# Gated linear recurrence and gated unit: 1024-token chunks, the gated input on GpSimd, the scan fed from PSUM, quarter-array convolution, 4 KB transfers

## Chip, cores, metric

The kernel runs on one core of a Trainium2 chip. The metric is the device time of one execution in microseconds, as the median of several. The kernel before takes 374.9 us (374.4 to 377.2 in three runs).

Engines are named as in the profile: PE is TensorE (PEld its weight loads), DVE is VectorE, ACT is ScalarE, POOL is GpSimd, SP issues the DMAs.

## The reference, cut to what matters

```python
B, S, D = 4, 6336, 256                      # 25,344 tokens, fp32 in and out
# recurrence, per channel
log_a = 8.0 * sigmoid(r_gate) * log(clip(sigmoid(a_param), 1e-6, 1 - 1e-6))
a     = exp(log_a)
xg    = sqrt(max(1 - a * a, 1e-6)) * sigmoid(i_gate) * x
h[t]  = a[t] * h[t-1] + xg[t]               # restarts at each of the 4 sequences
# gated unit on h
gate  = sigmoid(sum_k conv_w[k] * h[t - 4 + k])   # causal, 5 taps, per channel
out   = (gate * (h @ w_val)) @ w_out
```

Both kernels compute the sigmoids through tanh: sigmoid(z) is 0.5 * (1 + tanh(z / 2)).

## The kernel before: the parts that matter

Tokens go through in windows of 512. Inputs arrive with tokens on the partitions. The recurrence needs channels on the partitions, so TensorE transposes; u and tanh of r are transposed, and everything after that is channel-major. A list scheduler inside the kernel writes the order of the instructions.

```python
# loads: four rows of 1 KB per partition
nc.sync.dma_start(dst, src[t0:t0 + nj * P, :].rearrange("(j p) d -> p j d", p=P))
# tanh of both gates
nc.scalar.activation(out=tri, in_=ri, func=ACT.Tanh, scale=0.5)
# u = (1 + tanh_i) * x: one DVE instruction, both inputs in SBUF
nc.vector.scalar_tensor_tensor(out=uring, in0=tri[:, 1], scalar=1.0, in1=xt, op0=ALU.add, op1=ALU.mult)
# a = exp(k * tanh_r + k), read from the transposed PSUM tile, written densely
nc.scalar.activation(out=aring[.., h, 0:n], in_=srT[:, h, 0:n], func=ACT.Exp, scale=khf, bias=khf)
# a * a on GpSimd, then the square root on ACT
nc.gpsimd.tensor_tensor(out=ering, in0=a, in1=a, op=ALU.mult)
nc.scalar.activation(out=nring, in_=ering, func=ACT.Sqrt, scale=-0.25, bias=b025)
# xg = uT (PSUM) * norm (SBUF); then the scan, both tensor inputs in SBUF
nc.vector.tensor_tensor(out=xg, in0=uT, in1=nh, op=ALU.mult)
nc.vector.tensor_tensor_scan(out=yb, data0=aring, data1=xg, initial=.., op0=ALU.mult, op1=ALU.add)
# convolution: ten matmuls of 128x128 diagonal weights, 512 wide
nc.tensor.matmul(out=gp[:, h, c0:c1], lhsT=diag[:, h, kk, :], rhs=yb[:, h, o:o + c1 - c0], ..)
```

Of the kernel before, what the change touches and what calls it, by code (L numbers as in the profile page):

```python
# [8 lines left out]
P = 128  # L9
WIN = 512  # L10
SUB = WIN // P
CONV_K = 5
C_SCALE = 8.0
NS = 11
NY = 7
NIN = 3
NTRI = 3
NOSB = 3
MIN_UNIT = [1, 2, 3, 4]
COST = dict(load=4.5, tanh=1.9, u2=1.3, srT=0.5, uT=0.5, exp=1.45, e=2.15, xg=0.66, scan=2.7, conv=2.4, tg=0.97,  # L20
            val=0.95, gv=1.16, out=0.47, osbD=0.64, osbA=0.62, sq=0.88, sq0=0.2, table=1.3, store=1.5,
            sem=0.15, dma=2.2)
FP32 = mybir.dt.float32
# [5 lines left out]
def make_plan(frac):  # L29




    nw = len(frac)
    nq = [max(1, round(2 * f)) for f in frac]
    qwin = [(g, i) for g in range(nw) for i in range(nq[g])]
    qlast = [sum(nq[:g + 1]) - 1 for g in range(nw)]
    done, nxt, free = {}, {}, {}
    order, units = [], []
    mode = "E"  # L40

    def at(op):
        return nxt.get(op, 0)

    while True:
        cands = []

        def cand(op, eng, dur, deps, prio, i, n=1):
            t = 0.0
            for d in deps:  # L50
                if d[1] < 0:
                    continue
                if d not in done:
                    return
                t = max(t, done[d] + COST["sem"])
            if eng == "ACT" and op != "osb" and (op == "sq") != (mode == "S"):
                dur = dur + COST["table"]
            cands.append((max(free.get(eng, 0.0), t), prio, op, eng, dur, i, n))

        def per_window(op, eng, prio, deps, limit=nw):  # L60
            g = at(op)
            if g < limit:
                cand(op, eng, COST[op] * frac[g], [(d, g + o) for d, o in deps], prio, g)

        nsq = at("sq")
        per_window("load", "DMA", 0, [("tanh", -NIN), ("u2", -NIN)])
        per_window("tanh", "ACT", 3, [("load", 0), ("srT", -NTRI), ("u2", -NTRI)])
        per_window("u2", "DVE", 0, [("tanh", 0), ("uT", -NS)])
        per_window("srT", "PE", 0, [("tanh", 0), ("exp", -2)])
        per_window("exp", "ACT", 1, [("srT", 0), ("scan", -NS), ("e", -NS)])  # L70
        per_window("e", "POOL", 0, [("exp", 0), ("xg", -NS)])
        per_window("uT", "PE", 1, [("u2", 0), ("xg", -1)], nsq)
        per_window("xg", "DVE", 3, [("uT", 0), ("sq", 0), ("scan", -1)], nsq)
        per_window("scan", "DVE", 2, [("xg", 0), ("val", -NY)], nsq)
        per_window("conv", "PE", 3, [("scan", 0), ("tg", -1)])
        per_window("tg", "ACT", 0, [("conv", 0), ("gv", -2)])
        per_window("val", "PE", 2, [("conv", 0), ("gv", -1)])
        g = at("gv")
        if g < nw:
            cand("gv", "DVE", COST["gv"] * frac[g],  # L80
                 [("tg", g), ("val", g), ("out", qlast[g - 2] if g >= 2 else -1)], 1, g)
        q = at("out")
        if q < len(qwin):
            cand("out", "PE", COST["out"], [("gv", qwin[q][0]), ("osb", q - 1)], 1, q)
        q = at("osb")
        if q < len(qwin):
            for e, eng in (("D", "DVE"), ("A", "ACT")):
                cand("osb", eng, COST["osb" + e], [("out", q), ("store", qwin[q][0] - NOSB)], 0.5, q)
        g = at("store")
        if g < nw:  # L90
            cand("store", "DMA", COST["store"] * frac[g], [("osb", qlast[g])], -1, g)

        n = at("e") - nsq
        if n and mode == "E":
            all_in = at("exp") == nw
            stuck = at("e") == at("exp") and (all_in or ("scan", at("exp") - NS) not in done
                                              and at("exp") >= NS)
            low = (nsq - at("scan")) * (COST["xg"] + COST["scan"]) <= 2 * COST["table"] + COST["sq"] * n
            enough = n >= min(MIN_UNIT[min(len(units), len(MIN_UNIT) - 1)], nw - nsq)
            if stuck or (low and enough):  # L100
                cand("sq", "ACT", COST["sq0"] + COST["sq"] * sum(frac[nsq:nsq + n]),
                     [("e", nsq + n - 1)], -1, nsq, n)
        if not cands:
            break
        t, prio, op, eng, dur, i, n = min(cands)
        free[eng] = t + dur
        order.append((t, op, i, eng, n))
        nxt[op] = i + n
        for k in range(i, i + n):
            done[(op, k)] = t + dur + (COST["dma"] if eng == "DMA" else 0.0)  # L110
        if op == "sq":
            units.append(n)
        if eng == "ACT" and op != "osb":
            mode = "S" if op == "sq" else "E"
    assert at("store") == nw
    order.sort(key=lambda o: o[0])
    return order, qwin
# [3 lines left out]
def kernel(  # L121
# [15 lines left out]
    T = B * S  # L137

# [4 lines left out]

    nwin = (T + WIN - 1) // WIN
    ntok = [min(WIN, T - g * WIN) for g in range(nwin)]

    segs = []
    for g in range(nwin):
        t0, t1 = g * WIN, g * WIN + ntok[g]
        cuts = [t0] + [c for c in range(S, T, S) if t0 < c < t1] + [t1]  # L150
        segs.append([(c0 - t0, c1 - t0, c0 % S == 0) for c0, c1 in zip(cuts[:-1], cuts[1:])])
    YW = WIN + 4 * max(len(s) for s in segs)

    plan, qwin = make_plan([n / WIN for n in ntok])

    const = ctx.enter_context(tc.tile_pool(name="const", bufs=1))
    inp = ctx.enter_context(tc.tile_pool(name="inp", bufs=3))
    live = {}

    def load(g):  # L160
        nj = ntok[g] // P
        t0 = g * WIN
        ri = inp.tile([P, 2, SUB, D], FP32, name="ri", tag="ri", bufs=NIN)
        xt = inp.tile([P, SUB, D], FP32, name="xt", tag="xt", bufs=NIN)
        for dst, src in ((ri[:, 0, 0:nj, :], rf), (ri[:, 1, 0:nj, :], if_), (xt[:, 0:nj, :], xf)):
            nc.sync.dma_start(dst, src[t0:t0 + nj * P, :].rearrange("(j p) d -> p j d", p=P))
        live["ri", g], live["xt", g] = ri, xt

    with tc.manual_schedule():
        ap2 = const.tile([H, P], FP32, name="ap2")  # L170
        nc.sync.dma_start(ap2[:], a_param.rearrange("(h p) -> h p", p=P))
        wrow = const.tile([CONV_K, D], FP32, name="wrow")
        nc.sync.dma_start(wrow[:], moe_conv_w[:, :])
        for g in range(NIN):
            load(g)
# [7 lines left out]
        wv = const.tile([P, H, D], BF16, name="wv")  # L183
        nc.gpsimd.dma_start(wv[:], moe_w_val.rearrange("(hk p) n -> p hk n", p=P))
        wo = const.tile([P, H, D], BF16, name="wo")
        nc.gpsimd.dma_start(wo[:], moe_w_out.rearrange("(hk p) n -> p hk n", p=P))
        khf = const.tile([P, H], FP32, name="khf")
        wcol = const.tile([P, H, CONV_K], FP32, name="wcol")
        with tc.tile_pool(name="ps_setup", bufs=1, space=bass.MemoryType.PSUM) as ps_setup:
            kps = ps_setup.tile([P, H], FP32, name="kps")  # L190
            nc.tensor.transpose(out=kps[:], in_=ap2[0:H, :], identity=ident_f[0:H, 0:H])
            kt = const.tile([P, H], FP32, name="kt")
            nc.scalar.activation(out=kt[:], in_=kps[:], func=ACT.Tanh, scale=0.5)
            ksig = const.tile([P, H], FP32, name="ksig")
            nc.vector.tensor_scalar(out=ksig[:], in0=kt[:], scalar1=0.5, scalar2=0.5,
                                    op0=ALU.mult, op1=ALU.add)
            nc.vector.tensor_scalar(out=ksig[:], in0=ksig[:], scalar1=1e-6, scalar2=1.0 - 1e-6,
                                    op0=ALU.max, op1=ALU.min)
            kln = const.tile([P, H], FP32, name="kln")
            nc.scalar.activation(out=kln[:], in_=ksig[:], func=ACT.Ln)  # L200
            nc.vector.tensor_scalar(out=khf[:], in0=kln[:], scalar1=0.5 * C_SCALE, scalar2=None, op0=ALU.mult)
            wc_ps = ps_setup.tile([P, H, CONV_K], FP32, name="wc_ps")
            for h in range(H):
                nc.tensor.transpose(out=wc_ps[:, h, :], in_=wrow[0:CONV_K, h * P:(h + 1) * P],
                                    identity=ident_f[0:CONV_K, 0:CONV_K])
            nc.vector.tensor_copy(out=wcol[:], in_=wc_ps[:])
# [25 lines left out]
        def op_load(g, eng, n):  # L232
            if g >= NIN:
                load(g)
# [176 lines left out]
```

## Time and profile before

| | before |
|---|---|
| median time | 374.9 us |
| profiled span | 372.5 us |
| DVE busy | 334.6 us |
| ACT busy | 312.4 us |
| PE busy | 272.4 us |
| POOL busy | 138.3 us |
| DMA queue's share of 16 engines | 85.7% |

The busy line of the profile counts, for each engine, the time in which it works on an instruction. A group's line gives the source line, the engine and operation, what it writes and reads, how often, then the total busy time and the mean length of one in ns, then the idle time just before such instructions and who ended it. The lines on which the argument rests are in the prediction below.

These are the groups by shape of the kernel before; the second number behind the bar is the mean in ns.

```profile
L257 ACT ACTIVATE aring<-srT,khf 128x512 f32<-128x512 bf16 x98 | 70.7, 795 | 3.4 <-PE srT L228 2.2 <-issue 1.2
...
L257 ACT ACTIVATE aring<-srT,khf 128x256 f32<-128x256 bf16 x2 | 1.0, 562 | 0.0
```

### The profile page before, as it was taken

The numbers are of one execution on the slowest core, as the hardware profiler recorded it, in microseconds if no ns is written. First come the engines' busy times: TensorE is split into PE (matmuls) and PEld (weight loads), VectorE is DVE, ScalarE is ACT, GpSimd is POOL, SyncE is SP. The second block draws the span as 40 slices with busy tenths as digits, with TensorE's granted clock in tenths as the row PEclk, the third lists the DMA queues.
The fourth block names the chain that finished last, engine by engine and source line by source line (L and its number), as shares of the span: only waits on it lengthen the run. The fifth ranks groups of instructions, "written<-read, shape, count | busy, mean of one in ns | idle before, by whom it ended". The sixth has DMA issues, their size and how long they took to land.

```text
span 372.5 us, 5299 instructions
## 1 busy us (share of the span) xinstructions
PE 272.4 (73%) x1933; PEld 159.9 (43%) x1933; DVE 334.6 (90%) x326; ACT 312.4 (84%) x298; POOL 138.3 (37%) x111
## 2 busy tenths in 40 slices
PE   0362779877686969877677887696976696869994
PEld 0232445444445535434344454363543363435543
DVE  3363999999999979999999999999999999999982
ACT  4898899999998799998967989789997997873342
POOL 2234435634362726434425324451655056300000
PEclk9995699999899899999889989789999899999998
DMA  8999996999999989996889979979999895313333
GB/s 210 355 348 353 356 350 201 298 353 339 345 361 324 330 268 361 352 364 202 280 264 339 351 226 295 356 255 344 301 323 336 278 340 187 127 56 114 113 114 141
DMA packets 105160, 104.42 MB, mean 280 GB/s; under 512 B 3240, under 2 KB 105135, under 8 KB 105135
## 3 DMA queue, kind: packets, MB, share of 16 engines
q1 hardware_dynamic: 104590, 103.83, 85.7%
q0 software_dynamic: 544, 0.26, 0.5%
q8 instruction: 15, 0.25, 0.3%
q14 instruction: 11, 0.08, 0.1%
HBM read 78.39 MB, written 25.95 MB: 280 GB/s over the span
## 4 chain that ended last, share of the span: by engine, by line
DVE 34%; ACT 23%; issue 19%; PE 14%; DMA 5%; POOL 2%; DVEq 0%; ACTq 0%
DVE yring L306 13%; DVE uring L246 8%; DVE gv L344 7%; ACT tri L240 6%; ACT ering L277 5%; PE gp L321 5%; PE ops L356 4%; ACT aring L257 4%; DMA xt<-in_x_dram 3%; DVE xg L290 3%; PE val L338 3%; ACT tg L327 3%; DVE osb L367 2%; ACT L327 2%; ACT L277 2%
## 5 line engine op out<-in xcount | busy, mean ns | idle before, releaser
L262 POOL TENSOR_TENSOR ering<-aring 128x1024 f32<-128x1024 f32 (+1 forms) x50 | 105.7, 2121 | 140.9 <-ACT aring L257 121.8
L321 PE MATMUL gp<-yring,diag 128*128 128x512 bf16 (+4 forms) x530 | 124.5, 384 | 24.7 <-DVE yring L306 14.2
L306 DVE TENSOR_TENSOR_SCAN yring<-aring,yring,xg 128x512 bf16<-128x512 f32 (+4 forms) x98 | 139.5, 1464 | 0.7
L240 ACT ACTIVATE tri<-ri 128x2048 bf16<-128x2048 f32 (+1 forms) x50 | 94.4, 1907 | 0.0
L321 PEld LDWEIGHTS <-diag 128*128 128x128 bf16 x530 | 50.8, 102 | 83.5 <-issue 16.3
L356 PE MATMUL ops<-wo,gv 128*128 128x256 bf16 x396 | 61.8, 280 | 26.2 <-DVE gv L344 12.4
L257 ACT ACTIVATE aring<-srT,khf 128x512 f32<-128x512 bf16 (+1 forms) x100 | 71.8, 791 | 3.4 <-PE srT L228 2.2
L246 DVE SCALAR_TENSOR_TENSOR uring<-tri,xt 128x1024 bf16<-128x1024 bf16 (+1 forms) x50 | 67.4, 1356 | 7.0 <-ACT tri L240 6.9
L327 ACT ACTIVATE tg<-gp 128x1024 bf16<-128x1024 f32 (+1 forms) x50 | 51.1, 1023 | 25.7 <-PE gp L321 21.2
L344 DVE SCALAR_TENSOR_TENSOR gv<-tg,val 128x1024 bf16<-128x1024 bf16 (+1 forms) x50 | 59.7, 1194 | 2.5 <-PE val L338 1.7
L304 POOL COPY yring<-yring 128x8 bf16<-128x8 bf16 x49 | 31.6, 644 | 77.4 <-DVE yring L306 77.4
L356 PEld LDWEIGHTS <-gv 128*128 128x128 bf16 x396 | 36.7, 99 | 50.0 <-DVE gv L344 20.2
L338 PE MATMUL val<-yring,wv 128*128 128x512 bf16 (+4 forms) x212 | 52.1, 371 | 5.3 <-DVE gv L344 5.3
L228 PE MATMUL srT<-ident_b,tri 128*128 128x128 bf16 x396 | 33.4, 232 | 22.2 <-ACT tri L240 22.2
L277 ACT ACTIVATE ering<-ering,b 128x3072 bf16<-128x3072 f32 (+2 forms) x21 | 47.0, 2280 | 0.1
L369 ACT COPY osb<-ops 128x512 f32<-128x512 f32 x46 | 27.2, 592 | 22.2 <-PE ops L356 19.1
L367 DVE COPY osb<-ops 128x512 f32<-128x512 f32 x53 | 36.1, 682 | 9.2 <-PE ops L356 8.0
L228 PE MATMUL uT<-ident_b,uring 128*128 128x128 bf16 x396 | 33.3, 232 | 15.0 <-DVE xg L290 14.7
L228 PEld LDWEIGHTS <-tri 128*128 128x128 bf16 x396 | 27.0, 104 | 33.2 <-ACT tri L240 27.1
L290 DVE TENSOR_TENSOR xg<-uT,ering 128x1024 bf16<-128x1024 bf16 (+1 forms) x50 | 33.7, 675 | 6.2 <-ACT ering L277 6.2
L228 PEld LDWEIGHTS <-uring 128*128 128x128 bf16 x396 | 28.3, 104 | 20.0 <-issue 14.3
L338 PEld LDWEIGHTS <-wv 128*128 128x128 bf16 x212 | 19.9, 99 | 18.9 <-issue 6.6
(31 smaller groups left out, 53.3 us busy)
## 6 DMA issues: line engine op xcount, KB each, us to landing
ri<-in_r_gate_dram SPq DMA_DIRECT2D x49, 512.0 KB, 6.1
ri<-in_i_gate_dram SPq DMA_DIRECT2D x49, 512.0 KB, 7.4
xt<-in_x_dram SPq DMA_DIRECT2D x49, 512.0 KB, 7.3
out_dram<-osb SPq DMA_DIRECT2D x49, 512.0 KB, 4.6
ri<-in_r_gate_dram SPq DMA_DIRECT2D x1, 256.0 KB, 7.0
ri<-in_i_gate_dram SPq DMA_DIRECT2D x1, 256.0 KB, 7.2
xt<-in_x_dram SPq DMA_DIRECT2D x1, 256.0 KB, 6.6
out_dram<-osb SPq DMA_DIRECT2D x1, 256.0 KB
```

The costliest lines, as they stand in the source:

```text
L228: nc.tensor.transpose(out=dst[:, h, j * P:(j + 1) * P], in_=src[:, j, h * P:(h + 1) * P], identity=ident_b[:])
L240: nc.scalar.activation(out=tri[:, :, 0:nj, :], in_=ri[:, :, 0:nj, :], func=ACT.Tanh, scale=0.5)
L246: nc.vector.scalar_tensor_tensor(out=uring[:, g % NS, 0:nj, :], in0=tri[:, 1, 0:nj, :], scalar=1.0, in1=xt[:, 0:nj, :], op0=ALU.add, op1=A ...
L257: nc.scalar.activation(out=aring[:, g % NS, h, 0:ntok[g]], in_=srT[:, h, 0:ntok[g]], func=ACT.Exp, scale=khf[:, h:h + 1], bias=khf[:, h:h ...
L262: nc.gpsimd.tensor_tensor(out=ering[:, g % NS, :, 0:ntok[g]], in0=a, in1=a, op=ALU.mult)
L277: nc.scalar.activation(out=nring[:, sl:sl + k, 0:H * WIN], in_=ering[:, sl:sl + k].rearrange("p s h t -> p s (h t)"), func=ACT.Sqrt, scale ...
L306: nc.vector.tensor_tensor_scan(out=yb[:, h, o:o + c1 - c0], data0=aring[:, g % NS, h, c0:c1], data1=xg[:, h, c0:c1], initial=0.0 if fresh ...
L321: nc.tensor.matmul(out=gp[:, h, c0:c1], lhsT=diag[:, h, kk, :], rhs=yb[:, h, o:o + c1 - c0], start=(kk == 0), stop=(kk == CONV_K - 1))
L327: nc.scalar.activation(out=tg[:, :, 0:ntok[g]], in_=live.pop(("gp", g))[:, :, 0:ntok[g]], func=ACT.Tanh, scale=0.5)
L338: nc.tensor.matmul(out=val[:, m, c0:c1], lhsT=wv[:, hk, m * P:(m + 1) * P], rhs=yb[:, hk, o:o + c1 - c0], start=(hk == 0), stop=(hk == H - 1))
L344: nc.vector.scalar_tensor_tensor(out=gv[:, :, 0:ntok[g]], in0=live.pop(("tg", g))[:, :, 0:ntok[g]], scalar=1.0, in1=live.pop(("val", g))[: ...
L356: nc.tensor.matmul(out=ops[:, e, :], lhsT=gv[:, hk, p0:p0 + P], rhs=wo2[:, hk, :], start=(hk == 0), stop=(hk == H - 1))
```

## The change

The intent is to take work off the DVE, the busiest engine, to free what remains there of waiting for GpSimd, and to make transfers longer:

- u moves to GpSimd (from the fifth chunk on). There, a pass that adds one comes first and a plain product second.
- The product with the norm is formed in token order: the norm is transposed instead of u, the product is transposed by a matmul into fp32 PSUM, and the scan reads it there.
- The convolution uses 64x64 tiles of the array, four at a time.
- Partitions hold four consecutive tokens, so that a transfer's packet is 4 KB. Access patterns with a stride put the tokens in order again: in exp's output, in the norm's transposes, in the transposes ahead of the scan and in the output matmul.
- Chunks of 1024 tokens, a fixed list of instructions in place of the scheduler, PSUM banks assigned by hand.

The diff, cut to its core:

```diff
-            nc.sync.dma_start(dst, src[t0:t0 + nj * P, :].rearrange("(j p) d -> p j d", p=P))
+        return dram[start[c] + o:start[c] + o + n, :].rearrange("(p q) d -> p q d", q=n // P)
 ...
-            nc.vector.scalar_tensor_tensor(out=uring[..], in0=tri[:, 1, ..], scalar=1.0,
-                                           in1=xt[..], op0=ALU.add, op1=ALU.mult)
+        def op_s1(k, bank):
+            t = tri[:, c % NRI, 1, 0:CHUNKS[c] * H]
+            nc.gpsimd.tensor_scalar(out=t, in0=t, scalar1=1.0, scalar2=0.0, op0=ALU.add, op1=ALU.add)
+        def op_u(k, bank):
+            if c in U_DVE:          # chunks 0 to 3
+                nc.vector.scalar_tensor_tensor(out=u, in0=t, scalar=1.0, in1=xt, op0=ALU.add, op1=ALU.mult)
+            else:
+                nc.gpsimd.tensor_tensor(out=u, in0=t, in1=xt, op=ALU.mult)
 ...
+                src = src.rearrange("c (s q p) -> c s q p", p=P, q=q)
+                dst = dst.rearrange("c (s p q) -> c s q p", p=P, q=q)
+            nc.scalar.activation(out=dst, in_=src, func=ACT.Exp, ..)
 ...
+            nc.vector.tensor_tensor(out=v, in0=u, in1=nn, op=ALU.mult)     # v is u; nn: the transposed norm, in PSUM
+                    dst = pp[..].rearrange("c (p q) -> c q p", q=q)
+                        nc.tensor.matmul(out=dst[:, j, :], lhsT=u[..], rhs=ident_b[:], start=True, stop=True)
-                        data0=aring[..], data1=xg[:, h, c0:c1],
+            nc.vector.tensor_tensor_scan(out=yring[..], data0=aring[..], data1=pp[..], initial=prev, ..)
 ...
-                        nc.tensor.matmul(out=gp[:, h, c0:c1], lhsT=diag[:, h, kk, :], ..)
+                    for r, h, col in QUADS:
+                        nc.tensor.matmul(out=pp[col * HP:(col + 1) * HP, ..],
+                                         lhsT=diag[r * HP:(r + 1) * HP, h, kk, :], ..)
 ... (the fixed plan, buffers, setup: left out)
```

## The prediction

> **What bounds the kernel now.** I read the page's busy shares first, then the busy time in stretches of the span, then the groups of instructions by shape inside two of those stretches, then the timeline of two engines side by side. The busy line and the stretches:
>
> ```profile
> PE 272.4 (73%) x1933; PEld 159.9 (43%) x1933; DVE 334.6 (90%) x326; ACT 312.4 (84%) x298; POOL 138.3 (37%) x111
> ...
> q1 hardware_dynamic: 104590, 103.83, 85.7%
> ```
>
> ```profile
> 20.00:40.00 20.00, 9.99 (x68) 6.09 (x67) 11.12 (x11) 18.81 (x16) 7.71 (x5) 0.73 1.10 353
> 40.00:320.00 280.00, 216.94 (x1569) 127.47 (x1568) 272.03 (x249) 255.50 (x243) 123.15 (x86) 0.95 0.95 307
> 320.00:360.00 40.00, 34.42 (x227) 18.82 (x226) 39.10 (x43) 20.02 (x22) 3.25 (x11) 1.00 0.27 93
> ```
>
> The columns of the stretches are PE, weight loads, DVE, ACT and POOL busy, the granted clock, the DMA share and GB/s. From 40 to 360 us the DVE is busy 311.1 of 320 us: it is the bound. The DMA is nearly as full (0.95) until 320 us and then falls to 0.27: loads run up to eleven windows ahead, so the last 40 us are DVE work alone. Why the DVE needs 334.6 us shows in the scan, first between 100 and 280 us, then after 330 us, when GpSimd makes no more squares:
>
> ```profile
> L306 DVE TENSOR_TENSOR_SCAN yring<-aring,yring,xg 128x512 bf16<-128x512 f32 x48 | 74.4, 1590 | 0.4
> L246 DVE SCALAR_TENSOR_TENSOR uring<-tri,xt 128x1024 bf16<-128x1024 bf16 x27 | 37.1, 1380 | 0.4 <-ACT tri L240 0.4
> L344 DVE SCALAR_TENSOR_TENSOR gv<-tg,val 128x1024 bf16<-128x1024 bf16 x26 | 31.3, 1205 | 1.9 <-PE val L338 1.1 <-ACT tg L327 0.8
> ```
>
> ```profile
> L306 DVE TENSOR_TENSOR_SCAN yring<-aring,yring,xg 128x512 bf16<-128x512 f32 x12 | 14.7, 1267 | 0.0
> L344 DVE SCALAR_TENSOR_TENSOR gv<-tg,val 128x1024 bf16<-128x1024 bf16 x8 | 9.6, 1200 | 0.2 <-PE val L338 0.2
> L306 DVE TENSOR_TENSOR_SCAN yring<-aring,yring,xg 128x256 bf16<-128x256 f32 x2 | 1.4, 739 | 0.0
> ```
>
> The same 512-wide scan takes 1267 ns alone and 1590 ns on average beside GpSimd; gv does not change (1200 and 1205). The timelines of DVE and of POOL from 164 us show one case, two scans under two squares, 5.75 us instead of 2.5:
>
> ```profile
> 164.95 5.75 DVE L306 TENSOR_TENSOR_SCAN yring<-aring,yring,xg 128x512 bf16<-128x512 f32 x2
> ```
>
> ```profile
> 164.97 4.66 POOL L262 TENSOR_TENSOR ering<-aring 128x1024 f32<-128x1024 f32 x2 [2.15 <-ACT aring L257]
> ```
>
> **What the Trainium skill says.** (1) "SBUF — State Buffer", section "Who interferes with whom": a DVE instruction with two SBUF inputs contends with a GpSimd instruction that reads SBUF, the loser waits for the whole instruction, and one with at most one SBUF input does not contend. The trace agrees: scan and u (two SBUF inputs each) stretch, gv, xg and the output copy (one input from PSUM) keep 1205, 680 and 682 ns whether GpSimd works or not. (2) "DMA: Bandwidth & Descriptors", section "Why small descriptors are slow": a fixed cost per packet; its ceiling for 16 engines is 435 GB/s ("Where 436 GB/s comes from"). Packets of 1 KB took 46 ns at the median here (356 GB/s over 16 engines), 50 on average, which fits. (3) "TensorEngine Tiling (Array Packing)", section "Key Properties": four 64x64 tiles run in parallel, and changing the mode drains the array. The trace before has no tiles, so nothing here shows it. (4) "SBUF — State Buffer", section "Door 1", on cachelines: a stride beyond 16 bytes in SBUF or beyond 8 in PSUM costs rate. Before, everything is contiguous; no row shows it.
>
> **The change, part by part.** Units are tokens: 25,344 of them, two elements per token and partition.
>
> *DVE.* u leaves for GpSimd in all but the first four chunks: 50 x 1.35 = 67.4 us become about 6.4 (676, 1209, and twice 2276 ns by the same slope). The scan reads the coefficient from SBUF and the input from fp32 PSUM, so its lock is gone, and 1024 tokens go in one instruction: 739 ns at 256 and 1267 at 512 give 2.06 ns per element, so 2.32 us for 1024; 46 x 2.32 + 4 x 1.27 + 6 x 0.74 = 116 us, against 139.5. The product xg still has one SBUF and one PSUM operand in bf16, 48 x 0.68 + 3 x 0.42 = 34. gv is untouched, 60. Output copies: 36 of 1024 elements on the DVE (0.68 at 512, so about 1.22) = 44, against 36. With setup the DVE has 265 us instead of 334.6.
>
> *GpSimd.* Squares alone last 1892 ns for 1024 and 1038 for 512 elements: 1.67 ns per element and 0.18 fixed. 46 x 1.89 + 4 x 1.04 + 6 x 0.61 = 95 us. u at the same two-input rate is 3.60 us per 1024-token chunk, 21 such and three smaller: 80. The added "plus one" pass over the same tiles has one input; between half and the whole of u's rate: 43 to 80. The small copies of four columns (31.6 us, mostly waiting for the lock) go. Sum 218 to 255 us: 58 to 68% of the old span, off the bound.
>
> *ACT.* The same functions in longer instructions: tanh 1060 ns at 1024 and 1925 at 2048 give 3.66 at 4096, so 23 x 3.66 + 2 x 1.93 + 3 x 1.06 = 91 (94.4 before); exp 562 at 256, 795 at 512, so about 1.23 at 1024, 46 x 1.23 + 4 x 0.80 + 6 x 0.56 = 63 (71.8); square roots 16 instructions at 0.84 ns per element plus 0.27 each = 47; tg 51; 12 full output copies of 1.02 and two half ones = 13 (27.2); 25 table loads of 1.283 = 32. That is 297, less the overlap of neighbours: before, the groups add up to 326 and the busy time is 312, so 0.05 us per instruction, 169 instructions: 290 us. ACT becomes the busiest engine.
>
> *TensorE.* Start to start, matmuls in a row take 56 ns for 128 columns, 109 for 256, 216 for 512. Per 512 tokens before: 16 transposes 0.9, conv 10 x 216 = 2.2, val 0.9, out 0.9 = 4.8 us. After: 24 transposes 1.3, conv 20 quarter-array matmuls, in fours at once 5 x 216 = 1.1, val and out 1.7 = 4.1 us, some 205 us in all if the strided output of the last transpose is free, 270 to 300 if it is four times slower. PE stays below ACT, barely in the bad case.
>
> *DMA.* Rows of four tokens are contiguous, so a packet is 4 KB. Taking 46 ns for the first KB and 37.6 for each further one (the skill's ceiling), 159 ns: 412 GB/s, 252 us for 103.8 MB, 275 with the same excess of mean over median. But the loads' buffers now hold three chunks that tanh overwrites in place and GpSimd reads last, so loads can't run far ahead.
>
> *The sum.* ACT 290 us. Before the first tanh and after the last output copy it can't work: in the old trace it idles 5.9 us of the first 20 and 8.5 of the last 12.5; the small first and last chunks keep that near 15. Waits in between: the DVE, the bound before, idled 8 of 280 us (3%). Now DMA, DVE and perhaps PE lie within a tenth of ACT and the plan is fixed, so I take 4%, 12 us. Span 317; the timed median lies 2.4 us above the span (374.9 against 372.5): 319 us.
>
> **The rivals.** *DMA takes over.* Per three chunks 12.6 MB have to come and go in about 33 us, 381 GB/s, a rate that no slice of the old page reaches (364 at most). For it: share 0.95 before, shallower buffers, one issuing queue where loads wait behind stores. Against: packets four times as large. If packets come no faster, 319 us of pure transfer plus ends give 335 to 345.
>
> *Strides bite.* exp now writes fp32 at 16-byte steps, the last transpose writes PSUM at 16-byte steps, and weights are read at 8-byte steps. If exp ran at half rate, ACT would have 335 us and the kernel 360 or more. No row before tells; the choice of four tokens, just within the SBUF rule, suggests that somebody minded it. For PSUM it is outside the rule, but PE has room.
>
> *GpSimd is slower than thought.* A mixed bf16 and fp32 product may not run at 1.67 ns. At double the cost POOL reaches 330 us and sets the end near 350. I find this the least likely: two inputs already cost two cycles each pair.
>
> *Nothing in the way.* If ACT idles only at its ends, 305 us; if its long instructions overlap more, 300.
>
> **Range and chances.** The centre is 319. Below 303 ACT would have to beat its own sum. A DMA-bound run ends near 340. I take 303 to 339 for 8 in 10, and rest 3% on "within 2%" (above 367) and 1% on slower: that needs strides and DMA to go wrong together. Faster by over 2%: 0.96.
>
> **What will show it.** Right: scans of 1024 near 2.3 us, all alike, beside a busy POOL; DVE near 265, ACT near 290 us busy and over 88% of its span; packets near 160 to 170 ns. Wrong: exp well above 1.3 us or xgT matmuls above 100 ns start to start (strides); conv's fours in turn, not together (tiles); tanh waiting for DMA by more than 15 us in sum, and a DMA share of 0.95 (DMA); POOL above 80%. The prediction is most easily wrong by ACT stalls that the fixed plan turns into waits everywhere.

## The result and the profile after

The changed kernel takes 413.8 us (413.2 to 414.1 in four runs), against 375.0 in the same rounds. The ratio is 1.102, with a 95% interval of 1.098 to 1.106: 10% slower, where 15% faster was forecast. A ratio is the mean time of one kernel's fast runs over that of the other's fast runs of the same rounds, so it is not quite the ratio of the medians.

The page of the changed kernel: the busy line, three rows of its 40 equal slices (each digit is the busy share in tenths), and the DMA queue.

```profile
PE 279.3 (68%) x2947; PEld 197.8 (48%) x2987; DVE 260.0 (63%) x222; ACT 327.9 (80%) x192; POOL 340.2 (83%) x116
...
DVE  2451795448652798079844897189916377689973
ACT  7999989987928996599947992899845699768553
POOL 1235969999999999999999999999999999991000
...
q1 hardware_dynamic: 29968, 104.35, 68.7%
```

The DVE did lose what it was to lose (334.6 to 260.0 us), but POOL is now 90% busy or more in every slice from the seventh to the 36th, and the DVE and ACT have gaps everywhere. Busy time in the stretch from 80 to 360 us, in the columns of the prediction:

```profile
80.00:360.00 280.00, 191.46 (x2046) 136.50 (x2074) 178.91 (x136) 220.89 (x112) 279.20 (x84) 0.86 0.73 264
```

POOL works 279.2 of 280 us. What it does, and how the other instructions that the prediction sized came out, by shape:

```profile
L350 POOL TENSOR_SCALAR ri<-ri 128x2048 bf16<-128x2048 bf16 x21 | 148.7, 7085 | 1.6 <-ACT ri L299 1.5
L441 DVE TENSOR_TENSOR_SCAN yring<-aring,yring,pp 128x1024 bf16<-128x1024 f32 x46 | 107.5, 2342 | 18.0 <-PE pp L419 17.6
L336 ACT ACTIVATE aring<-pp,khf 128x1024 f32<-128x1024 bf16 x46 | 96.4, 2203 | 6.4 <-PE pp L315 6.4
L342 POOL TENSOR_TENSOR ering<-aring 128x1024 f32<-128x1024 f32 x46 | 86.5, 1895 | 17.1 <-ACT aring L336 16.9
L365 POOL TENSOR_TENSOR uring<-ri,xr 128x2048 bf16<-128x2048 bf16 x21 | 86.0, 4109 | 0.5
...
L336 ACT ACTIVATE aring<-pp,khf 128x256 f32<-128x256 bf16 x6 | 3.4, 580 | 2.4 <-PE pp L315 2.4
```

Two lines are far from the forecast. The pass that adds one (L350) takes 7085 ns for 2048 elements, 1.7 times the product that follows it (4109). And exp (L336) takes 2203 ns for 1024 elements where two dense ones of 512 took 1590 together. The scan (2342) is as forecast, and it no longer stretches beside POOL.

Who waits for whom, in us in total, times and the longest wait:

```profile
DVE uring L409 <- PE pp L388: 46.2, 13, 11.1
PEld L388 <- ACT ering L374: 45.4, 8, 10.8
ACT ering L374 <- POOL ering L342: 43.0, 7, 9.2
```

Read from the bottom: the square root waits for POOL's squares, the norm's transposes wait for the square root, the DVE's product waits for the transposes. One late engine at the head of the chain leaves each of the others idle for some 45 us in these waits alone. The timeline of POOL alone, at 214 us, shows how it gets late:

```profile
214.30 8.15 POOL L365 TENSOR_TENSOR uring<-ri,xr 128x2048 bf16<-128x2048 bf16 x2
222.42 7.08 POOL L350 TENSOR_SCALAR ri<-ri 128x2048 bf16<-128x2048 bf16 x1
229.59 4.12 POOL L365 TENSOR_TENSOR uring<-ri,xr 128x2048 bf16<-128x2048 bf16 x1
233.67 3.74 POOL L342 TENSOR_TENSOR ering<-aring 128x1024 f32<-128x1024 f32 x2
237.38 7.07 POOL L350 TENSOR_SCALAR ri<-ri 128x2048 bf16<-128x2048 bf16 x1
```

(Spans on POOL are rough in this profile, but the starts agree with them: from the start of this add-one pass at 222.42 to that of the next product at 229.59 are 7.17 us.) A chunk costs POOL 7.1 + 4.1 + 3.7 = 15 us. ACT needs some 13 us per chunk even with the slow exp: tanh 3.6, two exps 4.4, square root 1.8, two tanhs of the gate 2.1 and a third of two table loads 0.9.

### The profile page after: what moved, and what is told of

Same layout as the page of the kernel before. It is cut to its first block, busy times and chain, and to the rows that moved or that the text cites. A ratio compares the mean times of both kernels' runs of the same rounds, so it can differ in the third digit from the quotient of the medians.

```text
span 412.2 us, 7204 instructions
## 1 busy us (share of the span) xinstructions
PE 279.3 (68%) x2947; PEld 197.8 (48%) x2987; DVE 260.0 (63%) x222; ACT 327.9 (80%) x192; POOL 340.2 (83%) x116
## 4 chain that ended last, share of the span: by engine, by line
PE 21%; POOL 21%; issue 20%; ACT 17%; DMA 13%; DVE 5%; SPq 3%; POOLq 0%; ACTq 0%; DVEq 0%
POOL uring L365 8%; POOL ri L350 7%; PE pp L453 6%; DMA xr<-in_x_dram 6%; DMA ri<-in_i_gate_dram 6%; POOL ering L342 6%; ACT aring L336 5%; ACT ri L299 5%; PE pp L488 4%; PE pp L419 4%; ACT ering L374 3%; DVE yring L441 3%; PE pp L472 3%; PE pp L388 3%; SPq L221 2%
## 5 line engine op out<-in xcount | busy, mean ns | idle before, releaser
L350 POOL TENSOR_SCALAR ri<-ri 128x2048 bf16<-128x2048 bf16 (+2 forms) x24 | 156.2, 6512 | 1.6 <-ACT ri L299 1.5
L441 DVE TENSOR_TENSOR_SCAN yring<-aring,yring,pp 128x1024 bf16<-128x1024 f32 (+2 forms) x54 | 115.1, 2143 | 19.1 <-PE pp L419 18.8
L342 POOL TENSOR_TENSOR ering<-aring 128x1024 f32<-128x1024 f32 (+2 forms) x56 | 94.2, 1697 | 33.0 <-ACT aring L336 29.4
L336 ACT ACTIVATE aring<-pp,khf 128x1024 f32<-128x1024 bf16 (+2 forms) x56 | 104.7, 1963 | 9.3 <-PE pp L315 9.2
L299 ACT ACTIVATE ri<-ri 128x4096 bf16<-128x4096 f32 (+2 forms) x28 | 90.3, 3226 | 11.1 <-DMA ri<-in_i_gate_dram 10.8
L365 POOL TENSOR_TENSOR uring<-ri,xr 128x2048 bf16<-128x2048 bf16 (+2 forms) x24 | 90.5, 3782 | 3.1 <-PE pp L419 2.5
L478 DVE SCALAR_TENSOR_TENSOR gv<-tg,pp 128x1024 bf16<-128x1024 bf16 (+1 forms) x51 | 60.3, 1182 | 38.9 <-ACT tg L464 29.9
L453 PE MATMUL pp<-yring,diag 64*64 64x512 bf16 (+15 forms) x1196 | 72.4, 375 | 15.3 <-ACT tg L464 14.6
L419 PE MATMUL pp<-ident_b,uring 128*128 128x128 bf16 x396 | 56.5, 332 | 13.6 <-ACT aring L336 5.1
L488 PE MATMUL pp<-wo,gv 128*128 128x256 bf16 x396 | 54.5, 280 | 10.1 <-DVE gv L478 6.9
```

Of the source, the lines that this page charges most:

```text
L299: nc.scalar.activation(out=tri[:, c % NRI, :, 0:w], in_=src, func=ACT.Tanh, scale=0.5)
L336: nc.scalar.activation(out=dst, in_=src, func=ACT.Exp, scale=khf[:, h:h + 1], bias=khf[:, h:h + 1])
L342: nc.gpsimd.tensor_tensor(out=ering[:, c % NE, h * n:(h + 1) * n], in0=a, in1=a, op=ALU.mult)
L350: nc.gpsimd.tensor_scalar(out=t, in0=t, scalar1=1.0, scalar2=0.0, op0=ALU.add, op1=ALU.add)
L365: nc.gpsimd.tensor_tensor(out=u, in0=t, in1=xt, op=ALU.mult)
L419: nc.tensor.matmul(out=dst[:, j, :], lhsT=u[:, j * D + h * P:j * D + (h + 1) * P], rhs=ident_b[:], start=True, stop=True, skip_group_check ...
```

## Experiments

**Theory A**: the add-one pass on GpSimd, 156 us in all, sets the pace. **Theory B**: the strided exp on ACT does. **Theory C**: loads that can't run ahead do. The three can also follow one another, as one is removed.

### The pass left out, exp made dense, and both

The first kernel leaves the pass out, so that its result is wrong (u is tanh times x; the relative error, 0.916, is also what the reference gives off the chip when the one is left out from the fifth chunk on). The second lets exp walk the same elements in token order: it reads PSUM with a stride and writes SBUF densely. The result stays right. The third has both edits and is wrong.

```diff
 # first
-            nc.gpsimd.tensor_scalar(out=t, in0=t, scalar1=1.0, scalar2=0.0, op0=ALU.add, op1=ALU.add)
 # second
-                src = src.rearrange("c (s q p) -> c s q p", p=P, q=q)
-                dst = dst.rearrange("c (s p q) -> c s q p", p=P, q=q)
+                src = src.rearrange("c (s q p) -> c s p q", p=P, q=q)
+                dst = dst.rearrange("c (s p q) -> c s p q", p=P, q=q)
```

The pass left out:

> The GpSimd pass that adds one is left out, so the result is wrong on purpose; all else stays. Theory A (this pass, 156 us of a POOL that is 83% busy and over 99% from 80 to 360 us, sets the pace): POOL falls from 340 to about 185 us, and the time falls from 414 to 350-365 us, where ACT (328 us busy) ends it. Theory B (ACT's exp with its strided write, 2203 ns instead of 1230, sets the pace): no more than 3% faster, above 400 us. Theory C (loads that cannot run ahead): also above 400 us, with tanh waiting for DMA.

Exp dense:

> exp walks the same elements in token order: it reads PSUM with a stride of 128 elements and writes SBUF densely; the result stays right. If only the stride of the write costs, exp falls from 2203 to about 1230 ns and ACT from 328 to about 285 us busy; if a strided PSUM read costs as much, nothing moves. Theory A: the time stays within 2% of 414 us in either case, as POOL still sets the pace. Theory B: at or below 385 us.

Both:

> Both edits, result wrong on purpose. With the add-one pass gone and exp dense, ACT is the busiest at about 285 us. If the rest of my prediction holds: 303-330 us. If loads or the fixed plan bound it next (theory C): 340 us or more, with ACT below 85% of the span.

| kernel | median us | ratio to before (95%) |
|---|---|---|
| pass left out | 361.4 | 0.960 (0.953 to 0.967) |
| exp dense | 408.9 | 1.084 (1.075 to 1.093) |
| both | 325.5 | 0.867 (0.859 to 0.874) |

The busy lines without the pass, with the dense exp, and with both edits, in this order:

```profile
PE 268.7 (74%) x2947; PEld 190.4 (53%) x2987; DVE 257.4 (71%) x222; ACT 327.5 (91%) x192; POOL 186.1 (51%) x92
```

```profile
PE 271.7 (67%) x2947; PEld 194.5 (48%) x2987; DVE 255.8 (63%) x222; ACT 286.2 (70%) x192; POOL 340.0 (83%) x116
```

```profile
PE 259.0 (80%) x2947; PEld 186.0 (57%) x2987; DVE 255.2 (79%) x222; ACT 284.7 (88%) x192; POOL 185.2 (57%) x92
```

The groups by shape with the dense exp:

```profile
L336 ACT ACTIVATE aring<-pp,khf 128x1024 f32<-128x1024 bf16 x46 | 53.1, 1205 | 9.4 <-PE pp L315 9.4
...
L350 POOL TENSOR_SCALAR ri<-ri 128x2048 bf16<-128x2048 bf16 x21 | 148.8, 7089 | 0.9 <-ACT ri L299 0.9
```

Theory A holds for the kernel as it was changed. Without the pass 52 us go, and ACT is then busy for 91% of the span. With the dense exp alone ACT loses 42 us of work (327.9 to 286.2) and the time moves by 5 us only, because POOL is as full as before. The dense exp lasts 1205 ns, so the whole excess of 2203 ns came from the strided write; the read with a stride of 128 elements costs nothing that shows (without any stride, in a kernel below, exp takes 1203 ns). With both gone the time is 325.5 us. So the two costs lie behind each other: the second is worth 5 us while the first stands, and 36 us (361.4 to 325.5) once it has gone. Theory C had no run of its own; it is no more than a remainder here: with both gone, ACT waits 5 us for its loads.

### Which forms of the pass are long

The pass takes five forms in turn, chunk by chunk, each on a line of its own. This kernel also has a tile of ones and two output buffers instead of three.

> The add-one pass takes five forms in turn by chunk, each on a line of its own, result right: two ops (add, add) in place; one op (add); an add of a tile of ones (two tensor inputs); two ops out of place; mult then add. If the cost is the number of ops: the single op takes about half of 7085 ns; if it is the in-place write: the out-of-place one is short; if it is the tensor-scalar form on bf16 as such: all forms but the tensor of ones stay near 7 us, and that one takes about 4.1 us, as the product does.

```diff
+            f = c % 5
+            if f == 0:      # L354: two adds
+                nc.gpsimd.tensor_scalar(out=t, in0=t, scalar1=1.0, scalar2=0.0, op0=ALU.add, op1=ALU.add)
+            elif f == 1:    # L356: one add
+                nc.gpsimd.tensor_scalar(out=t, in0=t, scalar1=1.0, scalar2=None, op0=ALU.add)
+            elif f == 2:    # L358: a tile of ones
+                nc.gpsimd.tensor_tensor(out=t, in0=t, in1=ones, op=ALU.add)
+            elif f == 3:    # L360: two adds, out of place
+                nc.gpsimd.tensor_scalar(out=uring[..], in0=t, scalar1=1.0, scalar2=0.0, op0=ALU.add, op1=ALU.add)
+            else:           # L363: multiply, then add
+                nc.gpsimd.tensor_scalar(out=t, in0=t, scalar1=1.0, scalar2=1.0, op0=ALU.mult, op1=ALU.add)
```

POOL's groups by shape:

```profile
L360 POOL TENSOR_SCALAR uring<-ri 128x2048 bf16<-128x2048 bf16 x4 | 28.4, 7108 | 0.0
L354 POOL TENSOR_SCALAR ri<-ri 128x2048 bf16<-128x2048 bf16 x4 | 28.4, 7098 | 2.3 <-ACT ri L301 2.3
L356 POOL TENSOR_SCALAR ri<-ri 128x2048 bf16<-128x2048 bf16 x4 | 21.5, 5377 | 0.0
...
L358 POOL TENSOR_TENSOR ri<-ri,ones 128x2048 bf16<-128x2048 bf16 x4 | 16.3, 4076 | 0.0
L363 POOL TENSOR_SCALAR ri<-ri 128x2048 bf16<-128x2048 bf16 x5 | 9.5, 1904 | 1.5 <-ACT ri L301 1.5
```

It is neither the in-place write nor the number of ops: one add takes 5377 ns, adding a whole tile of ones 4076, and multiply-then-add 1904. No theory had expected the last. The result of this kernel was wrong (relative error 365), which was not intended. The out-of-place form writes into a ring slot that, in the order of the plan, transposes of an older chunk have yet to read: for chunks 18 and 23 the pass comes 9 and 10 operations before the second transposes of chunks 14 and 19, which share their slots. A replay off the chip bears this out: the reference, with just these two half chunks overwritten by that pass, is off by 365.1 in relative error (the norm of the difference over that of the reference), as was measured. The two output buffers are not to blame: the plan never has more than two in use. Other runs show right results with two adds, one add and multiply-then-add; the tile of ones and the out-of-place form were not run by themselves. The durations stand.

Five more in-place forms, on the kernel with the dense exp:

> Five more forms of the add-one pass, all in place and all right, one line each: add then multiply by 1; multiply by 1 then subtract -1; subtract -1 alone; add then max with -8; multiply then add. If only multiply-then-add has a short path: the others take 5 to 7 us. If an add as first op is what costs: the two that begin with multiply take 1.9 us. If two equal ops cost: only two adds are long.

```diff
+ f == 0 (L352): scalar1=1.0,  scalar2=1.0,  op0=ALU.add,  op1=ALU.mult
+ f == 1 (L354): scalar1=1.0,  scalar2=-1.0, op0=ALU.mult, op1=ALU.subtract
+ f == 2 (L356): scalar1=-1.0, scalar2=None, op0=ALU.subtract
+ f == 3 (L358): scalar1=1.0,  scalar2=-8.0, op0=ALU.add,  op1=ALU.max
+ f == 4 (L360): scalar1=1.0,  scalar2=1.0,  op0=ALU.mult, op1=ALU.add
```

```profile
L354 POOL TENSOR_SCALAR ri<-ri 128x2048 bf16<-128x2048 bf16 x4 | 28.4, 7104 | 0.0
L358 POOL TENSOR_SCALAR ri<-ri 128x2048 bf16<-128x2048 bf16 x4 | 28.4, 7091 | 0.3
L356 POOL TENSOR_SCALAR ri<-ri 128x2048 bf16<-128x2048 bf16 x4 | 21.5, 5379 | 0.0
L360 POOL TENSOR_SCALAR ri<-ri 128x2048 bf16<-128x2048 bf16 x5 | 9.5, 1904 | 1.0 <-ACT ri L299 0.9
L352 POOL TENSOR_SCALAR ri<-ri 128x2048 bf16<-128x2048 bf16 x4 | 7.6, 1899 | 0.0
```

The result is right. Of the forms tried, the pair of a multiply and an add is short in either order (1.9 us). A single add or subtract takes 5.4 us, and the three other pairs (two adds; multiply and subtract; add and maximum) 7.1 us. A single multiply was not tried, nor another type than bf16. So all three rules are wrong: what counts, among these forms, is the pair of ops as a whole. Why GpSimd treats this pair apart, the runs don't tell.

### The repair, and a dose between

Multiply by one and add one gives the same numbers. This kernel changes nothing else:

```diff
-            nc.gpsimd.tensor_scalar(out=t, in0=t, scalar1=1.0, scalar2=0.0, op0=ALU.add, op1=ALU.add)
+            nc.gpsimd.tensor_scalar(out=t, in0=t, scalar1=1.0, scalar2=1.0, op0=ALU.mult, op1=ALU.add)
```

> The add-one pass as multiply by 1 then add 1, on all chunks, nothing else changed. If the 1904 ns seen for this form is real work and right: correct result, POOL about 228 us busy, and the time as with the pass left out, 358-368 us, ended by ACT with its strided exp. If the form only looks short or is wrong: a wrong result (then the wrong result of the five-form kernel was its fault, not the out-of-place form's, which overwrites a ring slot too early).

It is right and takes 360.8 us (ratio 0.959, 0.953 to 0.966), as the kernel without the pass did (361.4). Its busy line:

```profile
PE 263.1 (74%) x2947; PEld 185.1 (52%) x2987; DVE 258.2 (72%) x222; ACT 327.2 (92%) x192; POOL 227.8 (64%) x116
```

Changing one operation name and one constant is worth 53 us. ACT with its strided exp is next. With the dense exp as well:

> Multiply-then-add pass and dense exp together, meant to be right and faster than both kernels: 323-332 us, as in the kernel with the pass left out and exp dense (325.5 us). If the 40 us of POOL work that come back matter after all: 335 us or more.

This kernel is right and takes 327.8 us over six runs; the four fast ones lie between 323.5 and 327.8, and two (328.9 and 332.9) count as slow by the rule for runs over 1.5% above the fastest (their granted clocks, 0.966 and 0.951, are hardly below the 0.960 to 0.966 of the fast ones). The ratio to before is 0.868 (0.862 to 0.874): it beats both kernels. Its profile was taken in a slow run, so only durations are read from it, no span: exp 1205 ns, the add-one pass 1898, the scan 2341, the same as in the fast runs of the other kernels.

For a dose between, the pass as a single add, on the kernel with the dense exp:

> A middle dose: dense exp, and the add-one pass as a single add (5377 ns seen in the five-form kernel, against 7089 for two adds and 1898 for multiply-then-add). POOL should be about 303 us busy, between 340 (408.9 us with dense exp) and 227 (327.8 us). If POOL's work is what the time follows, 36 us less than 408.9: 368-378 us, and POOL above 98% busy in the middle. If the time steps rather than follows (a fixed wait behind the slow pass): near 409 or near 328.

```diff
+            nc.gpsimd.tensor_scalar(out=t, in0=t, scalar1=1.0, scalar2=None, op0=ALU.add)
```

```profile
PE 269.4 (73%) x2947; PEld 192.5 (52%) x2987; DVE 255.7 (69%) x222; ACT 286.0 (77%) x192; POOL 302.2 (81%) x116
```

372.5 us (371.4 to 373.1), within the 368 to 378 expected. POOL's work fell by 37.8 us (340.0 to 302.2) and the time by 36.4 (408.9 to 372.5). While POOL is the bound, the time follows it nearly one to one.

### Were the other parts worth it?

Three more kernels each undo one part. The first starts from the kernel with the dense exp and gives u back to the DVE in all chunks:

```diff
-U_DVE = [0, 1, 2, 3]
+U_DVE = list(range(28))        # and no add-one pass for these
```

> u goes back to the DVE for all chunks, as scalar_tensor_tensor with two SBUF inputs, no add-one pass, exp dense: the offload to GpSimd alone is undone. Lock theory: u alone takes 2276 ns at 2048 elements, and up to 1.9 us more beside a square; DVE 256 + 55 + some 15 us of blocking, about 325 us busy, and the kernel 340-355 us. If POOL's remaining load did not matter and the DVE has slack: below 330 us. If the offload was no gain at all: equal to or below the kernel with both fixes.

It takes 364.8 us (ratio 0.972), 12% more than the repaired kernel's fast runs (mean 326.4 us), so in this plan the offload is worth its price once the pass is short. The groups by shape show the lock again:

```profile
L342 POOL TENSOR_TENSOR ering<-aring 128x1024 f32<-128x1024 f32 x46 | 90.6, 1988 | 182.3 <-ACT aring L336 156.4 <-DVE yring L443 13.9 <-DVE uring L365 12.0
...
L365 DVE SCALAR_TENSOR_TENSOR uring<-ri,xr 128x2048 bf16<-128x2048 bf16 x23 | 56.9, 2475 | 5.7 <-DMA xr<-in_x_dram 5.7
```

The squares take 1988 ns instead of 1895, and u takes 2475 ns, where it took 2280 in the kernel with the short pass alone. The expectation missed on both sides: the DVE was busy 306 us and not 325, and the time is 10 us above the range. From 40 to 320 us the DVE is busy 261 of 280 us, so it is close to being the bound again. ACT now waits 40 us for the convolution; that this comes of a plan made for another split is likely but not shown. How much of the 365 us a plan made for this split would save stays open.

The second starts from the kernel with the short pass and lays tokens out in rows of 1 KB again. All the strides go with it:

```diff
-        return dram[..].rearrange("(p q) d -> p q d", q=n // P)
+        return dram[..].rearrange("(q p) d -> p q d", q=n // P)
 # and "c (p q) -> c q p" becomes "c (q p) -> c q p" in the transposes and the output matmul; exp dense
```

> The short add-one pass, and tokens back in rows of 1 KB: transfers of 1 KB, and no strided access left in exp, the transposes or the output matmul. If the 4 KB transfers are needed at this pace: packets of 50 us per thousand again, 319 us of pure transfer, DMA share near 0.95, time 335-350 us. If they are not: at or below the time of the kernel with both fixes, 320-330 us, with less PE time because the last transpose writes PSUM densely (56 instead of 109 ns start to start).

332.6 us (ratio 0.885, 0.880 to 0.890), 2% above the repaired kernel's fast runs on the same chip, between the two forecasts (320 to 330 if 4 KB is not needed, 335 to 350 if it is). Its busy line and its DMA queue:

```profile
PE 245.4 (74%) x2947; PEld 166.8 (51%) x2987; DVE 254.6 (77%) x222; ACT 285.0 (86%) x192; POOL 226.8 (69%) x116
...
q1 hardware_dynamic: 105232, 104.35, 95.1%
```

The queue is at 95.1% of a span of 329.9 us, which is 314 us of all 16 engines' time; with 4 KB packets, in the kernel with the short pass alone, it was 78.1% of 356.7, or 279 us. So at this pace 1 KB packets nearly fill the engines. PE, in turn, needs some 14 us less than the 259.0 of the kernel with both edits, because the transposes ahead of the scan write PSUM densely: start to start they take 56 ns in a row, against 109 with the 16-byte steps. The layout with 4 KB transfers, its strides included, is a gain, but a small one: about 6 us between the fast runs, and one of the two runs of the repaired kernel that were set aside as slow took as long as these (332.9). What the transfers alone are worth was not separated.

The third starts from the repaired kernel and brings back the convolution with 128x128 weights:

```diff
-                    for r, h, col in QUADS:
-                        nc.tensor.matmul(out=pp[col * HP:(col + 1) * HP, b0 + d0:b0 + d1], lhsT=diag[r * HP:(r + 1) * HP, h, kk, :], ..)
+                        nc.tensor.matmul(out=pp[:, b0 + d0:b0 + d1], lhsT=diag[:, h, kk, :], ..)
 ... (the loop over h, and the weights' setup to match: left out)
```

> The kernel with both fixes, but the convolution again with 128x128 weights, ten 512-wide matmuls per 512 tokens instead of five fours of 64x64. If the fours run at once, this adds about 5 x 216 ns per 512 tokens, 50 us of PE work: PE near 305 us busy, above ACT's 285, and the kernel 335-350 us. If the tiles save nothing (fours in turn, drains at each change of mode): PE unchanged or less, and 322-330 us.

```profile
PE 299.3 (85%) x2353; PEld 211.7 (60%) x2389; DVE 256.3 (73%) x221; ACT 286.7 (81%) x192; POOL 227.0 (64%) x116
```

355.1 us (ratio 0.942): 29 us more than the repaired kernel, and 5 above the range. PE has 40 us more work (299.3 against 259.0 in the kernel with both edits), and ACT waits 33 us for the convolution. So the tiles do run at once: in the traces the matmuls of a four start 3 to 4 ns apart. They are a needed part of the gain. What a change between tiles and the whole array costs was not measured.

## Why the prediction was wrong, point by point

- **What bounds the kernel before; the lock.** Right as far as it was tested. The scan at 1024 elements took 2342 ns against the 2.32 us forecast, all alike beside a full POOL, and the DVE's sum came to 260.0 us against 265.
- **The step that failed: "between half and the whole of u's rate: 43 to 80".** The add-one pass took 156.2 us. One input was taken to cost no more than two; with these two ops it costs 1.7 times as much. The sum for POOL, "218 to 255 us", became 340.2, and with it went the claim that POOL is "off the bound": from 80 to 360 us it works 279.2 of 280 us. That the pass was the cause is shown: the time falls by 52 us without it, by 53 with another pair of ops, and by 36, from the kernel with the dense exp, with a pass 37.8 us shorter.
- **u on GpSimd.** A smaller miss in the same sum: 4109 ns and not 3.60 us, 90.5 us and not 80.
- **exp, "46 x 1.23".** Wrong for the strided write: 2203 ns, 104.7 us in all against 63. ACT came to 327.9 us and not 290. The rival "strides bite" named it and its size ("360 or more"; 361.4 measured with the pass left out), but the prediction gave it too little weight. It did not set the time of the changed kernel, since POOL did.
- **The rival "GpSimd is slower than thought".** The right engine for the wrong instruction, and it was called the least likely. It put the end near 350 us for 330 us of POOL; at 340.2 it was 413.8. The difference is that POOL's long stretch begins with the first add-one pass only at 39.5 us and its last product ends at 378.9, with 33 us of other engines' work behind it. A bound engine's busy time has to be laid between its own start and the drain after it.
- **TensorE.** Right in the parts: four tiles at once, and a strided PSUM output that costs twice (109 ns), not four times. The sum was too small: PE came to 279.3 us (259.0 with both edits), not some 205. The same counting gives 4.8 us per 512 tokens or 238 us for the kernel before, against 272.4 measured, so start-to-start times leave out some 34 us of what the profile calls busy. And "below ACT, barely in the bad case" did not follow from the prediction's own figures: 300 is above 290.
- **DMA.** Right: the median packet of 4 KB took 159 ns in the trace, as worked out. In the changed kernel ACT waited 10.8 us for loads, below the 15 that was named as a warning.
- **The chances.** 1% was put on slower, because "that needs strides and DMA to go wrong together". The add-one pass alone was enough: with exp dense the kernel still takes 408.9 us, 8% more than before, and with nothing but the pass repaired 360.8, 4% less. Three of the prediction's own signs of being wrong came true: exp above 1.3 us, the transposes ahead of the scan above 100 ns, POOL above 80% (83%). The cause it named as the easiest, stalls of ACT in a fixed plan, did appear, but POOL made them.
- **The sum.** With the two mis-sized terms repaired, the kernel takes 327.8 us; the prediction said 319, with a range of 303 to 339. That does not make the forecast right, since it was made for the kernel without the repairs, but it shows that the sum for ACT was sound: with both edits ACT works 284.7 us of a span of 323.7 and is idle for 39.0, against 290 and 27 forecast.

## What to carry to other kernels

When work moves to another engine, the instruction that will run there has to be timed in its exact form, with these ops, types and strides, before a plan is built on it. Here two spellings of "plus one" differ by 3.7 times. In a design in which all engines come out near equal, one mis-sized term becomes the bound, and the others' savings turn into waits. And a repair that gains nothing alone, such as the dense exp (5 us), may be worth 36 us once the bound in front of it has gone, so test such pairs together too.

## What the Trainium skill lacked or had wrong

- "GPSIMD Engine Reference", section "Engine selection", says that one-input elementwise work on GpSimd runs at roughly line rate. Here that holds, of the forms tried, for a multiply and an add together only: 1899 ns for 2048 elements. A single add or subtract took 5377 and 5379 ns, other pairs 7091 to 7108 ns, and a two-input product 4109 ns. No page has the times of this instruction on GpSimd by its ops.
- "SBUF — State Buffer", section "Door 1", gives four fp32 as the stride that is free within a 16-byte line. For ACT's fp32 writes it isn't: at 16-byte steps exp took 2203 ns instead of 1205 for 1024 elements. At 8-byte steps (the 256-token chunks) it took 580 ns, against 562 dense. What the same passage adds, that a line needs two hits, fits both.
- "PSUM — Partial Sum Buffer", section "Specifications", says that non-contiguous access slows matmuls. It does, and the size can be added: 109 ns instead of 56 from one 128-column transpose to the next, at 16-byte steps. No page says that ACT reads PSUM at 256-byte steps at full rate: exp took 1205 ns that way and 1203 densely.
